# A recurrent attention and a gated feed-forward in one kernel: a new written order for all engines, with new engine choices

## The chip, the cores and the metric

The kernel runs on one core of a Trainium2 chip. Its engines work side by side, each through its own list of instructions in order: TensorE (PE in the profile; its weight loads are PEld), VectorE (DVE), ScalarE (ACT), GpSimd (POOL) and SyncE (SP), which here only issues transfers. The metric is device time in microseconds (us) of one execution, lower is better. A profile is one more execution, recorded; its span runs from the first instruction to the last.

## The reference, cut to what matters

For 4 batches, 8 heads, 768 time steps and a head size of 48, a gated linear recurrence with a complex decay, and on its output a gated feed-forward layer over 3,072 tokens of width 384:

```python
mag = np.sqrt(a_re * a_re + a_im * a_im)
scale = np.minimum(mag, 0.999) / (mag + 1e-06)
a_re_n, a_im_n = (a_re * scale, a_im * scale)
for t in range(S):
    new_re = ar * S_re - ai * S_im
    new_im = ar * S_im + ai * S_re
    kv = np.einsum('bhd,bhe->bhde', k[:, :, t], v[:, :, t])
    S_re, S_im = (new_re + kv, new_im)
    y[:, :, t] = np.einsum('bhd,bhde->bhe', q[:, :, t], S_re)
...
x = np.ascontiguousarray(attn_out.transpose(0, 2, 1, 3)).reshape(B * S, H * D)
g = x @ w_gate
gelu = 0.5 * g * (1.0 + erf(g * inv_sqrt2))
val = x @ w_val
ffn_out = gelu * val @ w_out
res_gate = 1.0 / (1.0 + np.exp(-(x @ w_res)))
return (x + res_gate * ffn_out).astype(np.float32)
```

## The kernel before, in words

**Tiling.** The recurrence is done in blocks of 128 time steps. Two such blocks (c = 0 and 1) of one batch make a group; there are 12 groups p = 0 to 11, three rounds of four batches (p % 4 is the batch, p // 4 the round). The feed-forward works on units u = 0 to 7: units 0 to 3 are the groups 0 to 3 (256 tokens each), units 4 to 7 are pairs of groups (512 tokens each).

**Steps.** All work is cut into some 1,370 named steps. A name is a kind, a group or unit, and often a block: `CP0.1.0`. Each step is one instruction, or a few of one engine, with what it reads and writes. The kinds that this document speaks of:

- Loads on SP's queue, 192 KB each (lines 525 and 889): `Lar`, `Lai` (the decay's two parts), `Lq`, `Lk`, `Lvf`.
- Gates: squares `SQI` and `SQR` (ACT or DVE), their capped sum `ADD` (DVE, 573), logarithms `LNR` and `LM`, `EXR` (ACT), the tangent of the phase `TH` (DVE, 554), `ATN` (ACT), running sums over time by matmuls `CSL` (597) and `CST` (631), exponentials `EX` and `EI`, the phase brought to one turn by `OFF` (ACT or DVE, 642), `FR` and `ABS` (DVE), then `SIN` and `COS` (ACT). All ACT functions go through one helper, line 509.
- From one round to the next: small copies through DRAM on POOL's queue (`DR` 582, `DS` 585, `DE` 605, `DI` 608, `DT` 611) and a carried phase (`CRA`, `CRB` 679, then `CDA`, `CDB` 684, accumulating transfers on POOL's queue). `MM`, `MN`, `EN` and `EB` scale the carried state (DVE, POOL or ACT).
- Products: `QE`, `KE` (696) and `QR`, `KR` (704) on DVE.
- Attention: transposes `TP` (PE) and their copies `CP` (DVE or ACT) for p below 5, above that transposing transfers `QT`, `KT` on SP's queue (709); `AT` (PE, 748), `AM` (DVE, 751), `DK` (PE, 756), `MI` and `ED` (DVE), `Y` (PE, 796 and 799), `X` (DVE or ACT). `VC` casts a value block that `Lvf` brought (520).
- Feed-forward: `XT` and `XC`, or a transposing transfer `XD` (818), bring tokens to the right layout; `GP` and `VP` (PE, 837) are the gate and value products in slices f, `GE` the GELU (ACT), `HM` their product (DVE, 848), `RP` (PE, 852) and `SG` (ACT) the output gate, `OP` (PE, 862) the output product, `OT` (DVE, 867) and `RX` (DVE or POOL, 874) the gated sum with x, `ST` the store on SP's queue (877).
- Weights on POOL's queue: `Wg0` to `Wg3`, `Wv0` to `Wv3` (909), `Wr` (912), `Wo0` to `Wo2` (915). Two tiny POOL copies, `HOLDO` and `HOLDW` (901), read a loaded `ai` tile, so POOL's list waits there for that load.

**What sets the order.** A string, `ORDER`, lists every step by hand. A loop at the end of the kernel runs through it, and each engine's list is the order of its own steps in that string. A digit behind a name's colon is the buffer that the step's tile takes. The words `log`, `trig` and `gelu` load a set of ACT's function tables. A dictionary `PARAMS['eo']` says which engine does a step that has a choice.

```python
with tc.manual_schedule():
    for nm in ORDER(st) if callable(ORDER) else ORDER.split():
        if nm in tables:
            nc.scalar.preload_act_table_set(tables[nm])
        else:
            st.run(*nm.split(":"))
```

So an instruction that waits holds all that is behind it on its engine or queue.

Of the kernel before, what the change touches and what calls it, by code (L numbers as in the profile page):

```python
# [64 lines left out]
        'CP0.0.1': 'ACT',  # L65
        'CP0.1.0': 'DVE',
# [61 lines left out]
        'MN6': 'DVE',  # L128
# [53 lines left out]
        'SQI1': 'ACT',  # L182
# [9 lines left out]
        'SQI9': 'ACT',  # L192
# [4 lines left out]
        'SQR11': 'ACT',  # L197
        'SQR2': 'DVE',
        'SQR3': 'ACT',
        'SQR4': 'ACT',  # L200
# [4 lines left out]
        'SQR9': 'ACT',  # L205
        'VC0.0': 'DVE',
        'VC0.1': 'DVE',
        'VC1.0': 'POOL',
        'VC1.1': 'DVE',
        'VC10.0': 'POOL',  # L210
        'VC10.1': 'ACT',
        'VC11.0': 'DVE',
        'VC11.1': 'POOL',
        'VC2.0': 'POOL',
# [59 lines left out]
ADD3 log LM3 Lai5.1:3 Lai4.1:4 Lk1.0:1 FR1.1 KR0.1 QE0.0 QR0.0 LNR3 TP0.0.0:20 DK0.0 EXR3 Lar2.1:0 QE0.1 CP0.0.0 SQR4
TP0.0.1:11 OFF1.0 EX1.0 MI0:0 TH3 Lai4.0 AT0.0.0:00 QR0.1 DE1:0 HOLDO CRB1 DE0:1 FR1.0 ABS1 SQI4:3 CP0.0.1 ADD4
TP0.1.1:20 AT0.0.1:11 trig SIN1:1 AM0.0.1 CP0.1.1 COS1 AM0.0.0 SQR5 DR4:0 ATN3 Lai2.0:5 Lvf0.1:1 Lar2.0 Lk1.1 Lai5.0
Lai2.1 TP0.1.0:11 Y0.0:0 X0.0 SQR2 SQI2:1 log EI1.0 ADD2 CRB0 LM2 LNR2 AT0.1.1:10 CST3.1:3 CSL3.0:200 CSL3.1:0 AM0.1.1
SQI5:0 KE1 CP0.1.0 VC0.1 AT0.1.0:01 Lq1.0:1 Lq1.1 OFF3.1 KR1 AM0.1.0 LM4 EI3.1 EI3.0 EX3.0 FR3.1 QE1 CSL2.1:111 DK0.1
# [5 lines left out]
HM0.3 VP0.1:0 Lk2.1:2 trig ATN2 Lk2.0 HM0.1 VP0.5:3 Lk3.0:3 VP0.4:0 Y1.1:3 HM0.0 ATN4 ATN5 X1.1 HM0.4 HM0.5 CST2.1:2
DK1.1 CST2.0:0 HM0.2 OFF2.1 OFF2.0 XT1.1:31 OP0.1.0:1 FR2.1 FR2.0 ABS2 KE2 SIN3:0 XC1.1 OT0.1:0 XT1.0:2 Lq2.1:2 Lq2.0
SIN2:1 OP0.0.0:0 COS2 Lq3.0:3 Lq3.1 XC1.0 KR2 COS3 GP1.5:3 GP1.0:1 GP1.2:2 OT0.0:1 QE2 Lk3.1 QR2 gelu GE1.2 GE1.5
GE1.0 Lvf2.1:1 DS4.0 CDB0 CDB1 GP1.3:0 CRB2 GP1.4:2 QE3 QR3 GE1.3 GE1.4 CSL4.0:311 TP2.0.0:10 TP2.0.1:01 Lar6.1:1
Lar6.0 Lvf2.0:0 Lar9.1:0 Lai6.0:0 CP2.0.0 CP2.0.1 log EX4.0 VP1.0:2 CST4.0:1 AT2.0.0:10 EI4.0 AT2.0.1:01 TP2.1.1:00
LM5 KE3 HM1.0 ED1 OFF4.0 CP2.1.1 CSL5.0:300 EI5.0 Lai6.1 FR4.0 AM2.0.0 EX5.0 KR3 RP1.1:2 Lai7.1:1 VC2.1:2 VC2.0 DS5.0
VP1.5:1 TP2.1.0:01 gelu SG1.1 CST5.0:3 VP1.3:2 SQR6 CP2.1.0 SQI6:2 DI4 HM1.5 AM2.0.1 CRA4 OFF5.0 FR5.0 Y2.0:4 VP1.2:1  # L290
RP1.0:3 SG1.0 Lar7.0:3 Lar7.1 AT2.1.1:10 AT2.1.0:01 CDA4 HM1.3 SQR7 GP1.1:0 VP1.1:2 CSL5.1:3 DK2.0 X2.0 ADD6 HM1.2
AM2.1.1 GE1.1 HM1.1 VP1.4:1 AM2.1.0 MI2:0 Lai8.0:5 Lai7.0 log EX5.1 LNR6 ML4 ML5 ME5 EI5.1 DR6:0 CRA5 CDA5 CST4.1:0
CSL4.1:2 SQI7:1 EX4.1 Y2.1:5 HM1.4 OFF4.1 LM6 EXR6 RX0.0 Lq4.0:0 FR4.1 RX0.1 ADD7 Lvf3.1:1 Lar9.0 TP3.0.1:10 DT4.1:0
# [677 lines left out]
```

## Time and profile before

| what | us |
|---|---|
| median of 3 runs | 273.17 |
| lowest and highest of them | 271.66, 274.95 |
| the profiled execution, its own time | 271.67 |
| span of its instructions | 269.9 |

The profile's views used here: the page's busy time per engine, with the share of the span; stage windows, which give each engine's busy time in a stretch of the span, the granted clock of TensorE and the DMA engines' share; waits, which say who waited for whom, how long in total, how often and at the longest; the chain, which goes back from the last instruction through what released each step; and groups of instructions with mean or median durations. A queue's name ends in q: SPq is SP issuing transfers.

Where steps stand in time, from the order and the timeline: unit 0's products run from 49.6 to 60.7, its `OP` from 62.8 to 68.8; unit 3's `OP` from 133.3 to 137.4; unit 7's `OP` from 257.7 to 265.6. Weights are issued at 34.7 (`Wr`) to 41.6, and from 48.3 to 57.6 (`Wo2`).

### The profile page before, as it was taken

The page shows a single profiled execution, that of the slowest core. Times are in us where ns is not written, and L with a number is a line of the kernel's source. Part 1 is how long each engine was busy: PE and PEld are TensorE (multiplying, and loading weights), DVE is VectorE, ACT ScalarE, POOL GpSimd, SP SyncE. Part 2 cuts the span into 40 slices and gives each one's busy share as a digit, 9 for nine tenths or more (in the row PEclk, how much of TensorE's full clock was granted, in tenths as well). Part 3 has the DMA queues.
Part 4 walks back from the last instruction along what each step waited for, and adds up shares of the span by engine and source line. Part 5 has one row for each costly group of instructions (what it writes and reads, how often), then busy time and mean ns, then how long its engine had stood idle before and what let it go on. Part 6 is the DMA issues. An engine that isn't in the chain of part 4 may idle for free.

```text
span 269.9 us, 5310 instructions
## 1 busy us (share of the span) xinstructions
PE 233.5 (87%) x1926; PEld 146.6 (54%) x1926; DVE 221.8 (82%) x372; ACT 213.3 (79%) x340; POOL 104.3 (39%) x149
## 2 busy tenths in 40 slices
PE   0455576997989979999997999999999999999993
PEld 0212444774757677678643466645566455654461
DVE  1736989988899999999999999988988999534633
ACT  4799999896899999999998799979969983225320
POOL 4000291632105999455487166304940611040000
PEclk9995759999999999999999999999999999999999
DMA  7999999999893799979789925992975673521002
GB/s 154 216 224 215 214 190 186 183 185 187 173 205 62 153 196 191 218 153 184 173 162 240 228 51 113 183 216 57 195 132 132 156 164 82 90 87 58 2 29 87
DMA packets 170714, 41.35 MB, mean 153 GB/s; under 512 B 162624, under 2 KB 170688, under 8 KB 170688
## 3 DMA queue, kind: packets, MB, share of 16 engines
q1 hardware_dynamic: 163200, 37.04, 67.8%
q0 software_dynamic: 7488, 3.97, 11.2%
q8 instruction: 15, 0.25, 0.4%
q14 instruction: 11, 0.09, 0.1%
HBM read 31.33 MB, written 4.76 MB: 134 GB/s over the span
## 4 chain that ended last, share of the span: by engine, by line
PE 50%; DVE 23%; ACT 10%; DMA 6%; issue 6%; SPq 4%; DVEq 0%
PE gv L837 26%; PE sums L862 7%; PE sums L852 4%; PE sums L631 4%; SPq L525 4%; DVE h L848 3%; PE at L748 3%; PE sums L597 3%; DMA ai<-in_a_im_dram 3%; ACT L938 2%; DVE atm L751 2%; ACT ai L509 2%; ACT CS L509 2%; DVE padQ L704 2%; DMA k<-in_k_dram 2%
## 5 line engine op out<-in xcount | busy, mean ns | idle before, releaser
L837 PE MATMUL gv<-xT,wv 128*128 128x256 bf16 (+1 forms) x288 | 55.1, 325 | 2.8 <-DVE h L848 2.1
L848 DVE SCALAR_TENSOR_TENSOR h<-h,gv 128x512 bf16<-128x512 bf16 x72 | 47.3, 680 | 12.3 <-PE gv L837 12.1
L509 ACT ACTIVATE h<-gv 128x512 bf16<-128x512 f32 x72 | 40.7, 599 | 20.7 <-PE gv L837 20.0
L837 PE MATMUL gv<-xT,wg 128*128 128x256 bf16 (+1 forms) x288 | 54.1, 325 | 2.1 <-DMA out_dram<-ot 0.6
L862 PE MATMUL sums<-wo,h 128*128 128x384 bf16 x288 | 49.4, 326 | 1.6 <-DMA wo<-in_moe_w_out_dram 1.6
L938 ACT ACT_TABLE_LOAD x37 | 47.5, 1283 | 1.4 <-PEq L955 0.7
L837 PEld LDWEIGHTS <-wv 128*128 128x128 bf16 x288 | 27.1, 97 | 22.4 <-issue 5.5
L837 PEld LDWEIGHTS <-wg 128*128 128x128 bf16 x288 | 27.2, 97 | 21.0 <-issue 2.8
L862 PEld LDWEIGHTS <-h 128*128 128x128 bf16 x288 | 27.6, 98 | 19.8 <-issue 2.5
L751 DVE TENSOR_TENSOR atm<-at,mask 128x512 bf16<-128x512 f32 x48 | 32.1, 680 | 0.6 <-PE at L748 0.5
L509 ACT ACTIVATE ar<-ar 128x768 f32<-128x768 f32 x31 | 25.6, 846 | 0.1
L631 PE MATMUL sums<-ai,ut 128*128 128x384 f32 x40 | 19.2, 568 | 6.1 <-ACT ai L509 5.8
L867 DVE SCALAR_TENSOR_TENSOR ot<-sg,sums 128x384 f32<-128x384 f32 x24 | 12.9, 547 | 13.7 <-PE sums L862 10.7
L520 POOL CAST v<-vf 128x384 bf16<-128x384 f32 x13 | 12.2, 942 | 21.8 <-DMA vf<-in_v_dram 21.5
L597 PE MATMUL sums<-m,ut 128*128 128x384 f32 x24 | 11.1, 546 | 10.7 <-ACT m L509 10.1
L684 POOL DMA_DIRECT2D ai<-G x16 | 14.1, 886 | 14.8 <-DVE G L679 7.7
L509 ACT ACTIVATE sg<-sums 128x384 f32<-128x384 f32 x24 | 11.6, 496 | 8.3 <-PE sums L852 7.7
L585 POOL DMA_DIRECT2D m<-d x16 | 11.8, 771 | 12.9 <-DVE M L618 7.4
L852 PE MATMUL sums<-wr,xT 128*128 128x384 bf16 x72 | 15.1, 325 | 0.4 <-DVE h L848 0.4
L611 POOL DMA_DIRECT2D m<-d x16 | 13.3, 836 | 5.3 <-DMA d<-Ei 5.3
L679 POOL TENSOR_SCALAR G<-m 32x384 f32<-32x384 f32 x8 | 11.5, 1441 | 7.8 <-issue 5.1
L509 ACT ACTIVATE m<-m 96x8 f32<-96x8 f32 (+2 forms) x29 | 13.0, 468 | 1.5 <-DVE m L573 1.3
(93 smaller groups left out, 451.7 us busy)
## 6 DMA issues: line engine op xcount, KB each, us to landing
ar<-in_a_re_dram SPq DMA_DIRECT2D x24, 192.0 KB, 3.7
ai<-in_a_im_dram SPq DMA_DIRECT2D x24, 192.0 KB, 3.8
vf<-in_v_dram SPq DMA_DIRECT2D x24, 192.0 KB, 3.7
k<-in_k_dram SPq DMA_DIRECT2D x24, 192.0 KB, 3.8
q<-in_q_dram SPq DMA_DIRECT2D x24, 192.0 KB, 3.9
out_dram<-ot SPq DMA_DIRECT2D x24, 192.0 KB, 2.4
wv<-in_moe_w_val_dram POOLq DMA_DIRECT2D x4, 288.0 KB, 11.2
wg<-in_moe_w_gate_dram POOLq DMA_DIRECT2D x4, 288.0 KB, 11.2
```

Of the source, the lines that this page charges most:

```text
L509: return nc.scalar.activation(out=out, in_=in_, func=func, **kw)
L597: st.add("CSL%d.%d" % (p, c), "PE", lambda c=c: nc.tensor.matmul(out=st["csl", (p, c)], lhsT=lmat[c], rhs=part(("m2", p), (c,)), start=Tru ...
L611: st.add("DT%d.%d" % (p, u), "POOL", lambda u=u: nc.gpsimd.dma_start(out=st["m3", p][u * D:(u + 1) * D].rearrange("p r h -> p (r h)"), in_ ...
L631: return r + [nc.tensor.matmul(out=o, lhsT=tmat[c if s == 0 else 1], rhs=part(("ai", p), (c,)), start=not both, stop=True)]
L684: st.add("CD%s%d" % (nm, p), "POOL", lambda: nc.gpsimd.dma_start(out=part(("ai", pn), (cn,))[0:1], in_=row[127:128], accum_op=OP.add), r=[ ...
L751: st.add("AM" + sfx, "DVE", lambda: nc.vector.tensor_tensor(out=st["atm", i], in0=st["at", i], in1=mask4, op=OP.mult), r=[("at", i)], w=[( ...
L837: st.add("%sP%d.%d" % (nm.upper(), u, f), "PE", lambda f=f, fs=fs, nm=nm, w=w: [nc.tensor.matmul(out=st[nm + "p", (u, f)][:, j * 256:j * 2 ...
L848: st.add("HM%d.%d" % (u, f), "DVE", lambda f=f, h2=h2: nc.vector.scalar_tensor_tensor(out=h2(), in0=h2(), scalar=0.5, in1=gv(("vp", (u, f) ...
L852: st.add("RP%d.%d" % (u, jj), "PE", lambda jj=jj: [nc.tensor.matmul(out=st["rp", (u, jj)], lhsT=st["xT", u][:, i, jj * 128:(jj + 1) * 128] ...
L862: st.add("OP%d.%d.%d" % (u, jj, hh), "PE", lambda jj=jj, fs=fs: [nc.tensor.matmul(out=st["op", (u, jj)], lhsT=st["h2", u][:, f, jj * 128:( ...
L867: st.add("OT%d.%d" % (u, jj), "DVE", lambda jj=jj: nc.vector.scalar_tensor_tensor(out=st["ot", (u, jj)], in0=st["sg", u][:, jj], scalar=1. ...
L938: nc.scalar.preload_act_table_set(tables[nm])
```

## The change

Two things in the file differ: the text of `ORDER`, and entries of `PARAMS['eo']`. No function, size, buffer count or operation is changed; the set of steps is the same.

The counts of steps per engine that differ, before and after:

| kind | before | after |
|---|---|---|
| `SQI`, `SQR` | ACT 21, DVE 5 | ACT 12, DVE 14 |
| `CP` | ACT 6, DVE 14 | ACT 8, DVE 12 |
| `OFF` | ACT 9, DVE 15 | ACT 11, DVE 13 |
| `X` | ACT 14, DVE 10 | ACT 17, DVE 7 |
| `RX` | DVE 12, POOL 12 | DVE 8, POOL 16 |
| `VC` | ACT 5, DVE 6, POOL 13 | ACT 6, DVE 7, POOL 11 |
| `EB` | ACT 5, DVE 2, POOL 1 | ACT 2, DVE 1, POOL 5 |
| `CRA`, `CRB` | DVE 8, POOL 8 | ACT 3, DVE 5, POOL 8 |
| `EN` | DVE 2, POOL 6 | DVE 3, POOL 5 |
| table sets named | 37 | 36 |

One more table load stands ahead of the first ACT instruction of the new order, which begins with a square.

The diff, cut (`...` marks what is left out):

```diff
- 'CP0.0.1': 'ACT',
- 'CP0.1.0': 'DVE',
+ 'CP0.0.1': 'DVE',
+ 'CP0.1.0': 'ACT',
...
- 'SQI3': 'ACT',
- 'SQI4': 'ACT',
- 'SQI5': 'ACT',
+ 'SQI3': 'DVE',
+ 'SQI4': 'DVE',
+ 'SQI5': 'DVE',
...
 ORDER = """
-Lar1.1:0 Lar0.1:1 log LNR0.1:0 Lar0.0 Lai0.0:0 LNR0.0 SQR0.0 SQI0.0:0 ADD0.0 Lai0.1 SQI0.1 SQR0.1 ADD0.1 EXR0.1 TH0.1
...
+Lai0.0:0 SQI0.0:0 Lar1.1:0 Lar0.0:1 log LNR0.0:0 SQR0.0 Lai0.1 Lar0.1 EXR0.0 LNR0.1 EXR0.1 SQI0.1 ADD0.0 SQR0.1
...
```

The parts of each engine's list that the prediction speaks of. POOL's queue, before:

```text
DE1 HOLDO CRB1 DE0 DR4 Wr Wv1 Wg0 Wg2 Wg3 Wg1 DS4.1 Wv3 Wv0 DR5 DE2 Wv2 VC1.0 HOLDW Wo0 Wo1 DE3 DS5.1 Wo2 DS4.0 CDB0 CDB1 VC2.1 VC2.0
```

and after:

```text
CRB0 DE0 VC0.1 DE1 HOLDW Wg2 CRB1 DR4 Wg0 Wo2 Wg1 Wg3 Wr Wv2 Wv3 HOLDO DE3 DS4.1 Wv0 Wv1 DE2 Wo0 Wo1 DR5 CDB0 DS5.0 DS4.0 DS5.1 RX0.1 CDB1 VC3.0 DI4 CRA4 CDA4 DT4.1 VC2.1
```

DVE's list up to `ADD4`, before:

```text
SQR0.0 ADD0.0 SQI0.1 SQR0.1 ADD0.1 TH0.1 TH0.0 SQR1 ADD1 OFF0.0 FR0.0 ABS0.0 TH1 VC0.0 FR0.1 ABS0.1 KE0.0 KR0.0 KE0.1 OFF1.1 VC1.1 ADD3 FR1.1 KR0.1 QE0.0 QR0.0 QE0.1 CP0.0.0 MI0 TH3 QR0.1 FR1.0 ABS1 ADD4
```

and after:

```text
SQR0.0 SQI0.1 ADD0.0 SQR0.1 ADD0.1 TH0.0 TH0.1 SQI1 SQR1 ADD1 OFF0.0 SQI3 FR0.0 OFF0.1 FR0.1 ABS0.1 TH1 KE0.0 SQR2 ABS0.0 KE0.1 KR0.1 SQR3 KR0.0 ADD3 ADD2 QE0.1 QR0.1 SQR4 QE0.0 QR0.0 FR1.1 FR1.0 TH3 CP0.0.0 CP0.0.1 ABS1 SQI4 ADD4
```

SP's queue, the loads 20 to 50, before:

```text
Lar3.0 Lq0.0 Lar4.0 Lai5.1 Lai4.1 Lk1.0 Lar2.1 Lai4.0 Lai2.0 Lvf0.1 Lar2.0 Lk1.1 Lai5.0 Lai2.1 Lq1.0 Lq1.1 Lvf1.0 Lk2.1 Lk2.0 Lk3.0 Lq2.1 Lq2.0 Lq3.0 Lq3.1 Lk3.1 Lvf2.1 Lar6.1 Lar6.0 Lvf2.0 Lar9.1 Lai6.0
```

and after:

```text
Lai2.1 Lai2.0 Lar4.1 Lq1.0 Lq0.0 Lai4.1 Lar4.0 Lar5.0 Lk1.0 Lai5.0 Lai4.0 Lai5.1 Lk1.1 Lar5.1 Lq1.1 Lar7.0 Lvf1.0 Lvf1.1 Lk2.1 Lk2.0 Lvf2.0 Lq2.0 Lq2.1 Lq3.0 Lq3.1 Lk3.0 Lvf2.1 Lk3.1 Lar7.1 Lvf3.0 Lai7.1
```

Further on, SP's list before has `Lvf3.0 Lai9.1 ST0.0 Lq4.1 Lai8.1`; after, `Lk6.0 Lk4.1 ST0.1 Lvf3.1 Lk5.0`, with `ST0.0` behind group 5's first `XD`. PE's list has the same matmuls in another order; in both, `OP0.1` and `OP0.0` stand ahead of all of unit 1's products, and they read all three `Wo`.

More of the change, by code (lines that the diff above doesn't have):

```diff
@@ L127 @@
         'MN5': 'POOL',
-        'MN6': 'DVE',
+        'MN6': 'POOL',
         'MN7': 'POOL',
@@ L181 @@
         'SQI0.1': 'DVE',
-        'SQI1': 'ACT',
+        'SQI1': 'DVE',
         'SQI10': 'ACT',
@@ L191 @@
         'SQI8': 'ACT',
-        'SQI9': 'ACT',
+        'SQI9': 'DVE',
         'SQR0.0': 'DVE',
@@ L196 @@
         'SQR10': 'ACT',
[L197 removed]
+        'SQR11': 'DVE',
         'SQR2': 'DVE',
[L199 to L200 removed]
+        'SQR3': 'DVE',
+        'SQR4': 'DVE',
         'SQR5': 'ACT',
@@ L204 @@
         'SQR8': 'ACT',
[L205 to L208, printed above, removed]
+        'SQR9': 'DVE',
+        'VC0.0': 'ACT',
+        'VC0.1': 'POOL',
+        'VC1.0': 'DVE',
         'VC1.1': 'DVE',
[L210 to L214, printed above, removed]
+        'VC10.0': 'ACT',
+        'VC10.1': 'DVE',
+        'VC11.0': 'ACT',
+        'VC11.1': 'DVE',
+        'VC2.0': 'DVE',
         'VC2.1': 'POOL',
@@ L274 @@
[L274 to L278, printed above, removed]
@@ L284 @@
[L284 to L288, printed above, removed]
@@ L289 @@
[L289 to L293, printed above, removed]
@@ new lines @@
+FR0.1 ABS0.1 TH1 Lar3.0:2 Lk0.1 trig ATN1 Lvf0.1:1 Lar2.1:3 Lar2.0 Lar3.1 KE0.0 COS0.1:0 SIN0.0 SIN0.1 SQR2 ABS0.0
+CST1.0:0 CSL1.0:111 COS0.0 KE0.1 KR0.1 SQR3 KR0.0 ADD3 Lai2.1:3 Lai2.0 SQI2:3 ADD2 QE0.1 Lar4.1:1 Lq1.0:1 Lq0.0
+Lai4.1:4 CST1.1:2 CSL1.1:3 QR0.1 Lar4.0 SQR4 log EI1.0 LM3 QE0.0 Lar5.0:0 EX1.0 CRB0 DE0:0 QR0.0 TP0.0.0:10 EX1.1
+OFF1.0 OFF1.1 FR1.1 LNR3 EXR3 VC0.0:0 EI1.1 LM2 FR1.0 TH3 VC0.1 DE1:1 TP0.0.1:21 Lk1.0:1 Lai5.0:5 Lai4.0 CP0.0.0
+CP0.0.1 ABS1 CSL2.1:300 Lai5.1 HOLDW Lk1.1 AT0.0.1:00 DK0.0 AT0.0.0:11 TP0.1.1:01 SQI4:0 ADD4 Lar5.1 Lq1.1 AM0.0.1
@@ new lines @@
+CDB0 KR2 CRB2 ED1 GP1.4:3 Lq2.0:2 Lq2.1 QE2 OT0.0:1 Lq3.0:3 Lq3.1 Lk3.0:3 GE1.4 GP1.3:2 QR2 GE1.3 QE3 RP1.0:1 VP1.0:0
+SG1.0 DS5.0:1 DS4.0 DS5.1 CSL4.0:300 TP2.0.0:20 log EI4.0 ML5 LM5 QR3 EX4.0 HM1.0 CP2.0.0 Lvf2.1:0 TP2.0.1:11 CP2.0.1
+CSL4.1:0 Lk3.1 Lar7.1 KE3 KR3 CST4.0:2 DK2.0 EI4.1 EX4.1 AT2.0.1:00 CSL5.0:311 VP1.5:1 OFF4.0 EX5.0 EI5.0 SQR7 FR4.0
+Lvf3.0:1 RX0.0 HM1.5 AT2.0.0:11 TP2.1.1:01 Lai7.1:0 Lar6.1:0 Lar6.0 Lai6.1:2 Lai6.0 CP2.1.1 RX0.1 AM2.0.1 VP1.1:3
+AM2.0.0 CDB1 CST5.0:2 OFF5.0 TP2.1.0:10 Y2.0:4 SQR6 SQI6:2 ML4 Lq8.1:0 X2.0 CP2.1.0 VC3.0:3 DI4 CRA4 CDA4 DT4.1:0 ME4
@@ new lines @@
+HM1.1 FR5.0 MI2:0 ADD6 CSL5.1:0 VP1.2:3 VP1.4:2 AT2.1.0:00 AT2.1.1:11 AM2.1.0 AM2.1.1 Lvf4.0:1 Lai7.0 EX5.1 EI5.1
+SQI7:3 Lk4.0:0 Lar8.0:3 LNR6 VC2.1 DK2.1 VP1.3:1 XT2.0:00 Y2.1:5 XC2.0 HM1.3 HM1.4 CST4.1:0 EXR6 HM1.2 TP3.0.1:10
+RP1.1:2 TH6 ADD7 CRA5 DE4:4 X2.1 CP3.0.1 DT4.0 DR6:0 CDA5 OP1.0.0:3 gelu SG1.1 OFF4.1 FR4.1 AT3.0.1:00 TP3.0.0:21
+AM3.0.1 ED2 CP3.0.0 DI5 TP3.1.1:10 log ME5 ABS4 LM6 CST5.1:0 OT1.0:2 CP3.1.1 LNR7 Lar8.1 XT2.1:2 AT3.0.0:11 XC2.1
+AM3.0.0 OFF5.1 FR5.1 Lar9.1:1 Lk6.0:1 OP1.1.0:1 Lk4.1 ST0.1 DK3.0 GP2.3:3 Y3.0:6 EXR7 TP3.1.0:21 Lvf3.1:0 GP2.5:0
```

277 lines of the change are left out of this document (139 added, 138 removed).

## Prediction

> **What bounds the kernel now.** I read the page's busy totals first, then the stage windows, the waits, and the chain of waits. The page:
>
> ```profile
> PE 233.5 (87%) x1926; PEld 146.6 (54%) x1926; DVE 221.8 (82%) x372; ACT 213.3 (79%) x340; POOL 104.3 (39%) x149
> ```
>
> Three engines lie within 21 us of each other, so the average names no bound. By stage (columns: window, its length, then busy us of PE, PEld, DVE, ACT, POOL, TensorE's clock, DMA share, GB/s):
>
> ```profile
> 0.00:20.00 20.00, 6.74 (x10) 2.59 (x10) 8.53 (x21) 14.59 (x23) 4.00 (x15) 0.99 1.01 198
> 20.00:40.00 20.00, 12.21 (x71) 8.01 (x72) 16.50 (x29) 19.25 (x27) 7.84 (x11) 0.59 1.12 206
> 40.00:60.00 20.00, 16.83 (x180) 12.61 (x180) 18.98 (x31) 18.67 (x32) 8.23 (x14) 1.00 1.27 185
> 60.00:80.00 20.00, 17.73 (x158) 12.51 (x156) 17.62 (x27) 16.36 (x26) 3.83 (x6) 1.00 1.04 188
> 80.00:100.00 20.00, 18.35 (x209) 14.17 (x209) 19.90 (x36) 19.84 (x31) 15.39 (x20) 1.00 0.79 132
> 100.00:120.00 20.00, 19.33 (x204) 14.76 (x200) 19.87 (x33) 19.92 (x33) 13.18 (x19) 1.00 0.97 194
> ...
> 220.00:240.00 20.00, 20.00 (x192) 12.11 (x190) 13.31 (x23) 6.93 (x13) 2.95 (x5) 1.00 0.51 101
> ```
>
> The reader should see three regimes. Until 80 us PE waits (26.5 us idle) while the DMA engines are full. From 80 to 120, ACT and DVE are full and PE nearly. At the end PE alone is full. PE's work is the same in both kernels, so the end moves only by what PE's idle time loses.
>
> Inside the first regime, first two of the waits (who waited for what: us in total, times, longest), then three pieces of the chain (start, length, what):
>
> ```profile
> POOL v L520 <- DMA vf<-in_v_dram: 21.5, 5, 9.4
> ...
> PE sums L862 <- DMA wo<-in_moe_w_out_dram: 1.6, 1, 1.6
> ```
>
> ```profile
> 61.34 4.03 SPq L525
> ...
> 66.39 0.63 SPq L525
> ...
> 68.32 3.26 DMA ai<-in_a_im_dram
> ```
>
> An SP load issues every 0.6 to 1.2 us, but 4 to 5 us apart from 40.7 to 65.5. The packet records say why: from 36.3 to 64.9 us the weights' queue and the loads' queue move one packet each in turn, some 200 per us per queue, against 1,150 per us for loads alone. A load (1,024 packets of 192 bytes) then takes 5 us. The last weight (Wo2) lands at 65.8, and PE stands 1.62 us for it inside OP0.
>
> **The weights.** Before, DR4 waits for ADD4 (ends 33.93); eight weights follow at 34.72, four more from 48.3 to 56.9; the queue has no gap. In the new order one (Wg2) stands ahead of DR4; seven follow DR4, two DE3, two DE2. So 384 of the 4,992 weight packets go early, and the two DS5 copies no longer stand among the weights. If ADD4 ends when it did, 4,900 packets (weights and small copies) instead of 5,470 at 192 per us take 25.5 instead of 28.5 us: last landing 62.7 instead of 65.8.
>
> Does ADD4 end when it did? I added row durations along each queue. Ahead of ADD4 DVE has 4.7 us more medians (SQI1, SQI3, SQR2 to SQR4, ADD2, QE0.0 and others stand earlier or come from ACT). Before, DVE idles 14.6 us ahead of it, so there is room. SQR4 now waits for Lar4.0, SP's 26th load; the 26th was issued at 22.4 and loads land in 3.7, so SQR4 ends at 27.1. Behind it stand QE0.0 .74, QR0.0 .56, FR1.1 and FR1.0 .5 each, TH3 .95, two CP of .65, ABS1 .5, SQI4 and ADD4 .95 each: 34.0. Bounds: 33.9 (no delay) and 39.5 (none of the idle time used); I take 34.0, for each wait in that list has its source earlier.
>
> Start: ACT now squares first, and its log table load (rows: 1,283 ns), hidden before behind the first load's landing (ACT idle 2.67 us), stands after SQI0.0, from 4.7 to 6.0. It is covered: LM0.1 waits for ADD0.1 either way (9.4 before, 9.2 now). Cost 0; 1.3 without that cover.
>
> PE then: OP0.1 starts at 62.7, both OP0 take 3.9, then seven groups of .65, one of .49 and CSL4.0 .7: TP2.0.0 at 72.3, with 38.1 us of PE work ahead of it (row sums, overlap of neighbours left out). Before: 72.7, with 36.3. Lead: 0.4 + 1.8 = **2.2 us** (0 if ADD4 is at its late end, 4 if the weights are hidden whole).
>
> **Engine choices.** Counts from the two lists, by row means. ACT loses 5 SQI and 4 SQR (9 x .835), 3 EB (1.5) and one table set (1.28; the extra load at the start is idle time), and gains 2 CP (2.0), 2 OFF (1.2), 3 X (1.4), 1 VC (.5) and 3 CR: -3.7 net. CR has no ACT row; bounds .36 (DVE's CR) and .52 (ACT's 96x384 cast); I take .5, as it is ACT's. DVE gains 9 squares (.95 each) and loses 2 CP, 2 OFF, 4 RX, 3 X, 3 CR and some steps under .55: +1.5. POOL gains 4 RX (.97 each), 4 EB (.5) and loses 2 VC (.94) and small steps: +3.6. The squares move mostly before 45 us, where DVE has idle time. Between OP0.0 and OP3.0 (66.7 to 135.3, 68.6 us), the row sums of all that must precede a step, by data or by queue, grow by 63.9 for ACT instead of 64.7, and for DVE by about 63.2 instead of 64.3: **-0.8** (bounds 0 and -1.5).
>
> **SP's queue.** Before, ST0.0 stands ahead of Lq4.1 and waits for RX0.0:
>
> ```profile
> SPq L877 <- DVE ot L874: 37.4, 6, 17.3
> ```
>
> SP issues nothing from 80.6 to 88.3, and Lq4.1's landing is on the chain. Now ST0.0 stands behind unit 4's transposes, and ST0.1, in front, waits for POOL's RX0.1, which comes when OT0.1 (65.2) and three DS copies are through, by 69. PE idles 1.65 us from 80 to 100; I take half, **-0.8** (0 to -1.65). Some five loads get through beside the weights in either order; now Lq2, Lq3 and Lk3 are behind them and land by 68, at .9 each once the weights are done. Their readers QE3 and KE3 come at 70 and 73: 0. Without that margin, each late us is a us of DVE.
>
> **POOL's queue.** VC2.1 moves behind CRA4 (1.2), CDA4 (.8) and DT4.1 (.8), and PE's DK2.1, with VP1.3, Y2.1 and CST4.1 behind it, waits for VC2.1. FR4.0 at 75.5 gives VC2.1's end at 78.8; PE comes there at 81. Cover 2 us; DT4.1's wait for a landing can be 2.9 (longest of its line). DVE and POOL also collide:
>
> ```profile
> L520 DVE CAST Gb<-G x2: 349/1288/2226, 144.0 to 218.8; 96x384 bf16<-96x384 f32 x2
> ```
>
> The same cast takes 349 ns, and 2,226 at 143.96, beside POOL's VC7.0 and RX3.1. Two-input DVE rows hardly stretch: TH 970 on the mean, 947 median. So I give **+0.5** for both (0 to 2.4: 0.9 late for VC2.1, 1.5 for collisions). The Trainium skill ("SBUF — State Buffer", section "SBUF: two separate sides") says that the shared port pair is an exclusive lock for a whole instruction, also between a two-input DVE operation and a GpSimd one that reads SBUF. By that rule alone the added 3.6 us of POOL work could stop DVE for their whole length, and the sum below would be -0.2 instead of -3.3; the cast row agrees, the two-input rows do not.
>
> **Sum.** -2.2 - 0.8 - 0.8 + 0.5 = -3.3. The profiled execution took 271.67 (span 269.9 and 1.8 around it), so 268.4. The median of the three runs shown, 273.17, is 1.0055 of it: **269.9**. From 190 us on PE has 73.4 us of work and took 75; nothing is changed there.
>
> **Rivals.**
>
> *The lead is given back.* For: in 80 to 140 ACT, DVE and PE are all at 97% or more, DVE gets 1.5 us more, and VC2.1's place is tight. Against: ACT has less, PE's work there shrinks by what was done earlier. Price: -2.2 + 1.5 (all of DVE's) + 0.9 (VC2.1) - 0.8 = -0.6, so 271.1, or 272.6 by the median's scale.
>
> *Collisions at full length.* Every added us of POOL's elementwise work stops DVE, as in the cast row. Price: -3.3 - 0.5 + 3.6 = -0.2: 271.5, or 273.0. For: one row of six times its length. Against: the means of the HM and AM rows, 680 ns, are their medians. These two end within 1%. The lock of the Trainium skill's page "SBUF — State Buffer", above, would make this case the likeliest; the rows leave it the least.
>
> *Slower: ADD4 comes late.* DR4 holds seven weights behind a DVE that now has 4.7 us (with full-length squares 5.1) more to do. If the early waits leave it none of its 14.6 us, ADD4 ends at 39.5 and the last weight lands at 68.2; OP0, which is in front of all of unit 1 on PE, starts 5.4 later than before, less the 1.6 it stood: +3.8. With -0.8 from ACT: 274.7, or 276.2. It decides from ADD4 at about 38 us. For: the queues are in order, and Lar4.0 stands four places later in SP's. Against: the walk above.
>
> That the change does nothing is out: every engine's list differs.
>
> **Chances.** Forecast 0.53, given back 0.19, collisions 0.06, slower 0.22. About 1% is what a measurement here can tell from no change, 270.4 to 275.9. Of the forecast's own range (266 to 271.5) 0.07 lies above 270.4; of the slower case 0.02 lies under 275.9. Faster 0.46, same 0.34, slower 0.20. The range: at the low end all terms at their far ends (-4 -1.5 -1.65 = -7.2, so 264.5, or 266 scaled) and a little under, as PE's 26.5 idle us leave room: 264.5; at the high end the slower case: 277.
>
> **What would show it.** Right: a profile with ADD4's DVE instruction near 34, Wg2's issue before 28, the PE wait for wo ending at 63 or earlier, no hold of SP near 80 to 88, PE idle until 80 us near 23. Wrong: the first seven weights issued after 38; a PE wait for v or padK near 80; DVE casts of over 1 us; SP loads of 5 us whose readers wait; idle PE after 140, where I expect none new.

## The result, and the profile after

| | us | runs |
|---|---|---|
| before, median (lowest to highest) | 273.30 (271.66 to 274.95) | 20 |
| after, median (lowest to highest) | 275.19 (272.82 to 277.31) | 20 |
| after, the profiled execution (span) | 275.17 (273.4) | 1 |

After to before the ratio is 1.0066, 95% interval 1.0041 to 1.0091: 1.8 us slower, less than 1% but clear of the noise. I had forecast 269.9; the time lies inside my range of 264.5 to 277, on the other side of no change. Before's profiled execution, 271.67, was one of its fastest, after's an average one, so the spans differ by 3.5 us and the medians by 1.8.

The page after:

```profile
PE 235.8 (86%) x1913; PEld 147.5 (54%) x1926; DVE 229.3 (84%) x368; ACT 210.9 (77%) x339; POOL 108.7 (40%) x154
```

ACT lost 2.4 us (forecast 3.7), POOL gained 4.4 (3.6). DVE gained 7.5 where I had counted 1.5: its rows became longer. The stage windows after, and one of before that the prediction does not show:

```profile
20.00:40.00 20.00, 13.22 (x77) 8.74 (x78) 18.31 (x28) 18.92 (x29) 7.77 (x11) 0.79 1.04 189
40.00:60.00 20.00, 16.40 (x159) 11.38 (x157) 16.11 (x26) 17.29 (x28) 7.53 (x12) 0.95 1.27 188
60.00:80.00 20.00, 17.88 (x159) 13.27 (x160) 17.49 (x27) 18.05 (x28) 6.73 (x8) 1.00 1.03 181
...
140.00:160.00 20.00, 16.75 (x105) 8.57 (x109) 19.53 (x25) 15.27 (x28) 8.14 (x13) 1.00 1.01 190
```

```profile
140.00:160.00 20.00, 17.58 (x130) 9.41 (x130) 19.34 (x27) 16.38 (x32) 9.37 (x14) 1.00 0.90 192
```

From 40 to 60 PE, DVE and ACT all do less than before (16.8, 19.0 and 18.7 there): something none of them makes is late. From 140 to 160 DVE is full and PE has lost another 0.8 us against before. The chain says what was late first (start, length, what):

```profile
38.22 10.29 DMA wg<-in_moe_w_gate_dram
...
48.80 11.90 DMA wv<-in_moe_w_val_dram
...
60.74 0.84 PE gv L838 x6
```

and the waits between 55 and 70 us agree:

```profile
PEld L838 <- DMA wv<-in_moe_w_val_dram: 1.7, 1, 1.7
DVE h L849 <- PE gv L838: 1.7, 1, 1.7
PE gv L838 <- DMA wv<-in_moe_w_val_dram: 1.5, 1, 1.5
```

The wait for `wo` that the prediction started from is gone. PE stands for `wv` instead: `VP0.2` starts at 60.7 when Wv1 lands, against 51.9 before. `OP0.1` then starts at 65.8, not 62.7. The last weight, Wo1, was late as well (the issues of the three `Wo`, and their time to landing):

```profile
L916 POOL DMA_DIRECT2D wo<-in_moe_w_out_dram x3: 742/778/814, 37.4 to 54.8; - x3
...
DMA to landing us min/median/max: 9.0/10.6/11.3
```

Issued at 54.8, it lands at 66.1. `OP0.1` came to Wo1's slices at 66.4, so in this execution the value weights and the last landing were nearly level.

The second place is at 150 us; waits between 144 and 156, then the rows of the two lines that meet at 142, with the same K line before in between (counts; shortest, median and longest in ns; first and last start):

```profile
ACT sg L510 <- PE sums L853: 3.6, 1, 3.6
PEld L853 <- issue: 2.7, 1, 2.7
PE sums L853 <- DVE h L849: 2.4, 1, 2.4
```

```profile
L705 DVE TENSOR_TENSOR padK<-CS,kE x2: 958/1924/2889, 142.0 to 149.0; 128x1536 bf16<-128x1536 bf16 x2
L705 DVE TENSOR_TENSOR padQ<-CS,qE x2: 957/1212/1466, 146.4 to 152.7; 128x1536 bf16<-128x1536 bf16 x2
```

```profile
L704 DVE TENSOR_TENSOR padK<-CS,kE x2: 948/953/958, 143.1 to 149.5; 128x1536 bf16<-128x1536 bf16 x2
```

```profile
L875 POOL TENSOR_TENSOR ot<-ot,x x2: 917/922/927, 142.2 to 143.0; 128x384 f32<-128x384 f32 x2
```

`KR6` takes 2.89 us instead of 0.96 while POOL runs RX3.1 and RX3.0; `HM4.10`, behind it on DVE, comes late, and PE's `RP4.1`, which takes the buffer that `HM4.10` reads, stands 2.44 us for it until 152.3.

To see where the end was lost I read off when PE had done a given sum of its own work (row medians of before, along each kernel's own PE list). The last three columns are runs told below:

| PE's work done, us | before | after | RX3 on DVE | Wo2 last | best version |
|---|---|---|---|---|---|
| 29 (in unit 0's `OP`) | 64.1 | 66.3 | 65.3 | 61.8 | 61.9 |
| 32 (unit 0's `OP` done) | 68.4 | 69.5 | 68.4 | 65.3 | 66.2 |
| 45 | 82.8 | 84.0 | 82.9 | 79.9 | 80.1 |
| 85 | 125.6 | 127.1 | 126.0 | 123.1 | 123.2 |
| 109 | 152.6 | 155.3 | 151.8 | 152.0 | 149.0 |
| 117 | 160.6 | 164.0 | 161.5 | 160.0 | 157.8 |
| 221 (unit 7's last `OP`) | 263.3 | 266.7 | 265.3 | 263.1 | 260.9 |

The first row lies ahead of the 1.6 us for which PE stands for Wo2 in the kernel before (64.2 to 65.8), so its 2.2 us are too much. When unit 0 is done, after is 1.1 us behind; it loses 0.4 from there to 85 and 1.9 from 85 to 117. Behind that, nothing.

### The profile page after: what moved, and what is told of

The parts are those of the page before. It is cut to its first block, busy times and chain, and to the rows that moved or that the text cites. A ratio compares the mean times of both kernels' runs of the same rounds, so it can differ in the third digit from the quotient of the medians.

```text
span 273.4 us, 5296 instructions
## 1 busy us (share of the span) xinstructions
PE 235.8 (86%) x1913; PEld 147.5 (54%) x1926; DVE 229.3 (84%) x368; ACT 210.9 (77%) x339; POOL 108.7 (40%) x154
## 4 chain that ended last, share of the span: by engine, by line
PE 44%; DMA 18%; DVE 11%; ACT 11%; issue 6%; SPq 6%; POOL 2%; DVEq 0%; ACTq 0%; POOLq 0%
PE gv L838 19%; PE sums L863 13%; SPq L526 5%; DMA wv<-in_moe_w_val_dram 4%; DMA wg<-in_moe_w_gate_dram 4%; DMA ar<-in_a_re_dram 3%; PE sums L853 3%; ACT L939 2%; DMA ai<-in_a_im_dram 2%; PE sums L632 2%; PE sums L598 2%; ACT m L510 2%; PE at L749 2%; ACT ar L510 2%; ACT CS L510 1%
## 5 line engine op out<-in xcount | busy, mean ns | idle before, releaser
L838 PE MATMUL gv<-xT,wv 128*128 128x256 bf16 (+1 forms) x281 | 54.3, 324 | 2.4 <-DMA wv<-in_moe_w_val_dram 1.9
L838 PE MATMUL gv<-xT,wg 128*128 128x256 bf16 (+1 forms) x282 | 52.1, 324 | 2.4 <-DMA xT<-x 0.8
L510 ACT ACTIVATE h<-gv 128x512 bf16<-128x512 f32 x72 | 40.0, 601 | 13.9 <-PE gv L838 13.2
L838 PEld LDWEIGHTS <-wg 128*128 128x128 bf16 x288 | 27.5, 98 | 20.8 <-issue 1.9
L875 POOL TENSOR_TENSOR ot<-ot,x 128x384 f32<-128x384 f32 x16 | 18.4, 1151 | 47.8 <-DVE ot L868 47.7
L510 ACT ACTIVATE ar<-ar 128x768 f32<-128x768 f32 x27 | 22.6, 849 | 0.1
L685 POOL DMA_DIRECT2D ai<-G x16 | 13.3, 830 | 22.5 <-ACT ai L510 16.3
L598 PE MATMUL sums<-m,lt 128*128 128x384 f32 x24 | 12.4, 603 | 9.1 <-ACT m L510 9.1
L680 POOL TENSOR_SCALAR G<-m 32x384 f32<-32x384 f32 x8 | 10.8, 1355 | 22.4 <-DVE m L646 13.8
L632 PE MATMUL sums<-ai,ut 128*128 128x384 f32 x40 | 18.5, 547 | 0.6 <-DVE m L646 0.5
L705 DVE TENSOR_TENSOR padK<-CS,kE 128x1536 bf16<-128x1536 bf16 (+1 forms) x13 | 14.6, 1122 | 0.5
```

What stands on the lines that cost most here:

```text
L510: return nc.scalar.activation(out=out, in_=in_, func=func, **kw)
L598: st.add("CSL%d.%d" % (p, c), "PE", lambda c=c: nc.tensor.matmul(out=st["csl", (p, c)], lhsT=lmat[c], rhs=part(("m2", p), (c,)), start=Tru ...
L632: return r + [nc.tensor.matmul(out=o, lhsT=tmat[c if s == 0 else 1], rhs=part(("ai", p), (c,)), start=not both, stop=True)]
L705: return nc.vector.tensor_tensor(out=pad, in0=st["CS", p][:, cs[0] * H:(cs[-1] + 1) * H], in1=sb, op=OP.mult)
L838: st.add("%sP%d.%d" % (nm.upper(), u, f), "PE", lambda f=f, fs=fs, nm=nm, w=w: [nc.tensor.matmul(out=st[nm + "p", (u, f)][:, j * 256:j * 2 ...
L875: st.add("RX%d.%d" % (u, jj), rese, lambda jj=jj, pc=(p, c), eng=eng: eng.tensor_tensor(out=st["ot", (u, jj)], in0=st["ot", (u, jj)], in1= ...
```

## The experiments

Ratios are to the kernel before, run beside each on the same chip. Ten were made from the changed kernel (1.0066), three from the kernel before.

### Wo2 last (e1)

```diff
-FR3.0 ABS3 Wg0 Wo2 Wg1 Wg3 ...
+FR3.0 ABS3 Wg0 Wg1 Wg3 ...
-... VP0.4:2 Wo1 Y1.1:3 ...
+... VP0.4:2 Wo1 Wo2 Y1.1:3 ...
```

> The changed kernel with one weight moved: Wo2 goes from the third place behind DR4 to the last place of the weights, so that Wv0 and Wv1 come one place (384 packets of 768 bytes) earlier. Theory V (the value weights are late): in the changed kernel VP0.2 stands until 60.7 us for Wv1 and OP0.1 starts at 65.8 although all of Wo has landed by then. At some 200 packets per us Wv1 lands 1.9 us earlier, VP0.2 starts near 58.8 and OP0.0 ends near 67.6 instead of 69.5; if two thirds of that lasts to the end, the time is about 1.3 us lower than the changed kernel's 275.2, so 273.9. Rival L (only the last landing counts): the last weight lands as before, near 64, and OP0.1, which needs all twelve, ends no earlier; no change, 275.2. Rival E (the engines' backlog holds unit 0): VP0.2 starts earlier and OP0.0 does not; no change.

Measured: 271.18, ratio 0.9931 (0.9910 to 0.9953). One transfer moved takes the changed kernel from slower than before to faster, by 1.35% of the time. Waits between 55 and 70, and two windows:

```profile
PE sums L863 <- DMA wo<-in_moe_w_out_dram: 0.4, 1, 0.4
```

```profile
40.00:60.00 20.00, 17.54 (x189) 13.56 (x188) 17.93 (x30) 19.36 (x29) 6.04 (x9) 0.96 1.27 185
60.00:80.00 20.00, 18.29 (x162) 13.09 (x161) 18.27 (x29) 18.39 (x31) 8.97 (x11) 1.00 1.07 196
```

The wait for `wv` is gone, a short one for `wo` is back, and the three engines do more again from 40 to 60. Wv1 lands at 54.8 (60.7 after; 58.5 in the run with RX3 on DVE, whose order is the same up to there), `OP0.0` ends at 65.3 (69.5; 68.4). Theory V holds, and the gain is more than my 1.3, which counted Wo2 as 384 packets; it has 512. Up to 2 us of the 4.2 between the two profiles came from the start of the weights (34.6 here, 36.7 after), which differs between executions of the same order. Rival L is settled by two later profiles that differ in Wo2's place alone, both with RX3 on DVE (e3 and e5 below): the last weight lands at 63.7 in one and 63.9 in the other, but unit 0 is done at 68.4 with Wo2 third and at 66.3 with Wo2 last, and the ratios are 0.9999 and 0.9943.

### Six weights ahead of DR4 (e2)

```diff
-... EXR2 DR4:0 TP1.0.0:31 ...
+... EXR2 Wg0 Wg1 Wg3 Wr Wv2 Wv3 DR4:0 TP1.0.0:31 ...
```

> The changed kernel with Wg0, Wg1, Wg3, Wr, Wv2 and Wv3 moved ahead of DR4, so that they no longer wait for ADD4 (which ends at 35.7 us). They are issued from about 31.5 us. Theory H (the wait for ADD4 is what makes the weights late): the weights start some 5 to 7 us earlier and Wv1 lands near 55; OP0.0 ends 2 to 3.5 us earlier and the time is 273.0 (1.5 to 3 lower than 275.2). Rival S (the wait shields the loads): beside the weights a load takes 5 us instead of 1; five or six loads land later by up to 7 us each, units 0 and 1 get their inputs late, and what VP0.2 gains is lost ahead of it: 275 to 277.

Measured: 278.05, ratio 1.0191 (1.0154 to 1.0228). Rival S. The chain and a wait:

```profile
34.43 15.37 DMA vf<-in_v_dram
```

```profile
PE sums L632 <- ACT xT L520: 6.1, 1, 6.1
```

A load of v is 15.4 us on the chain, stuck beside the weights; DVE does nothing from 38 to 42, and PE stands 6.1. So the wait for ADD4, which I had priced as a risk, shields the loads.

### RX3.0 and RX3.1 on DVE (e3)

```diff
-        'RX3.0': 'POOL',
-        'RX3.1': 'POOL',
+        'RX3.0': 'DVE',
+        'RX3.1': 'DVE',
```

> The changed kernel with RX3.0 and RX3.1 on DVE instead of POOL. In the changed kernel the DVE row KR6 takes 2.89 us instead of 0.96 while POOL runs RX3.1, RX3.0 and CDB4, and QE6 and QR6 take 1.47 each beside POOL's EB6, DS8.1 and EN7. Theory C (the bf16 two-input DVE rows stand while POOL reads or writes the on-chip memory): KR6 is back near 1.0, DVE does 1.1 to 1.4 us of RX more and 1.9 less in KR6; PE's idle 2.44 us at 152.3 falls to about 1.5, and the time is lower by 0.5 to 1, 274.4. If POOL's rows then move forward and meet other DVE rows, the gain is smaller. Rival B (KR6 is long for another reason, and DVE's own sum is what counts): DVE has 1.1 to 1.4 us more, KR6 stays long, and the time goes up by about 1 us, 276.2.

Measured: 272.88, ratio 0.9999 (0.9968 to 1.0031), 1.8 us under the changed kernel. Groups of instructions between 132 and 160 us (busy, mean ns of one, idle before):

```profile
L752 DVE TENSOR_TENSOR atm<-at,mask 128x512 bf16<-128x512 f32 x6 | 3.8, 680 | 0.0
L705 DVE TENSOR_TENSOR padQ<-CS,qE 128x1536 bf16<-128x1536 bf16 x2 | 2.4, 1212 | 0.1
...
L705 DVE TENSOR_TENSOR padK<-CS,kE 128x1536 bf16<-128x1536 bf16 x2 | 2.1, 1026 | 0.2
```

padK's mean falls from 1924 to 1026; padQ, which stands beside POOL's `EB6` and `EN7`, is as it was. Theory C, and twice what I expected.

### Wg2 behind DR4 (e4)

```diff
-... AM0.0.0 Wg2 CRB1 ...
+... AM0.0.0 CRB1 ...
-... EXR2 DR4:0 TP1.0.0:31 ...
+... EXR2 DR4:0 Wg2 TP1.0.0:31 ...
```

> The changed kernel with Wg2 moved from ahead of CRB1 to just behind DR4, where the others stand. Theory S2 (the early weight slows the loads that ADD4 waits for: between 30 and 33 us only 1,644 load packets move instead of some 3,200, and Lk1.1 takes 2.8 us): Lai4's load lands up to 1.4 us earlier, SQI4 no longer waits 0.5, ADD4 ends 0.5 to 1 earlier; but Wv1 stands 384 packets further back, +1.9, so VP0.2 starts 1 to 1.4 later: time 275.2 to 276.2. Rival G (the early weight is a plain gain): ADD4 as it was, VP0.2 1.9 later, time 276.5.

Measured: 273.48, ratio 1.0015 (0.9989 to 1.0041): not slower, as both theories had it, but 1.4 us faster than the changed kernel, with intervals that just touch. The packet records show what makes up for the later place: the loads, no longer slowed at 30 to 33, get so far ahead that their queue is all but empty from 39 to 47 (SP waits for a v buffer), and there the weights move 240 to 268 packets per us instead of 200. Wv1 lands at 58.0, though it stands one weight further back (60.7 after; 58.5 in both e3 and e8, which have Wg2 early). Where the 1.4 us come from is not shown: unit 0 is done at 68.1, between e3's 68.4 and e8's 67.6. The early weight, which I had counted as a gain, is none.

### The parts that I had priced: SP's hold, squares, late RX

Before, with one store moved twice:

```diff
-... Lvf3.0:0 Lai9.1:2 ST0.0 Lq4.1 ...
+... Lvf3.0:0 Lai9.1:2 Lq4.1 ...
+... Lk7.0:2 ST0.1 ST0.0 Lq8.1:3 ...     (first run)
+... QE4 Lai9.0 ST0.0 Y3.0:6 ...         (second run)
```

> The kernel before with one store moved: ST0.0 goes from ahead of Lq4.1 to behind ST0.1, so that SP no longer stands 7.8 us (80.6 to 88.3) for RX0.0 with eleven loads behind it. The prediction's step: the load Lq4.1 and those behind it come up to 8 us earlier, PE loses up to 1.65 us less between 80 and 100, I took 0.8: 272.1 against 272.9. Rival (covered): the readers of these loads (KE4, QE4, QR4) stand behind DVE's own full list at 80 to 120 and would run no earlier; 272.9, within 0.3.

Measured: 279.31, ratio 1.0223 (1.0192 to 1.0255). Loads came 6.5 to 7.9 us earlier, and every DVE row up to 96 us kept exactly its distance (0.5) to before. Then:

```profile
DVE ot L867 <- DMA out_dram<-ot: 3.6, 1, 3.6
```

`OT1.1` takes the buffer that `ST0.0` empties, so the later store held DVE. That spoils the run as a test of the end, so the store was put where it goes out on time:

> The kernel before, with ST0.0 behind Lai9.0 instead of ahead of Lq4.1: the seven loads from Lq4.1 to Lai9.0 come 7 to 8 us earlier, while the store itself goes out when it did (88 us), so that OT1.1, which takes the store's buffer, is not held as it was (3.6 us) with the store behind ST0.1. The prediction's step: 0.8 lower, 272.2. Rival (covered: with the store behind ST0.1 the same loads came as early, and every DVE row up to 95 us kept its distance): 273.0, within 0.3; and if the loads behind Lai9.0 come earlier as well, not before Lvf4.0's own wait (93.0 us).

Measured: 274.02, ratio 1.0032 (1.0006 to 1.0058). No gain: the loads came 5.4 to 6.9 us earlier, the DVE rows up to 97 us again kept their distance (0.5), so the hold of 7.8 us was covered.

The changed kernel with nine squares back on ACT (`'SQI1': 'ACT'` and so on):

> The changed kernel with the nine squares that went to DVE (SQI1, 3, 4, 5, 9, SQR3, 4, 9, 11) back on ACT, their places in the order kept. DVE loses 8.6 us of work, ACT gains 7.5, six of the nine before 45 us. The prediction's step (they cost DVE nothing there, and ACT is worth 0.8 between units 0 and 3): the front is later, as ACT has 18.9 of 20 us in 20 to 40, by 1 to 3 us, and the middle by up to 2: 276.5 to 279. Rival D (DVE's list is what makes ADD4 and the weights late): ADD4 ends near 33, the weights start 1 to 2 us earlier, 273.5 to 275.

Measured: 277.04 (three runs), ratio 1.0136 (1.0114 to 1.0158), 1.9 us over the changed kernel. The squares are better on DVE, as the prediction had it.

The changed kernel with the ten RX of units 4 to 7 back:

> The changed kernel with the ten RX steps of units 4 to 7 that the change moved between DVE and POOL back where they were (seven on DVE, three on POOL). The rows KR9 and KE11, stretched by 0.55 and 0.68 beside RX4.0 and RX5.1, are then short. Theory F (from 165 us on PE has no gap, so nothing that DVE and POOL do there moves the end): 275.2, within 0.4; only the last rows (RX7.1, RX6) could move the tail, by 0.3. Rival (collisions count there too): 274.0; or DVE's 3 to 4 us more cost in the tail: 276.

Measured: 275.41, ratio 1.0087 (1.0057 to 1.0118), no difference to the changed kernel, in whose profile PE has no gap of over 0.25 us from 165 us on. In this run's profile it has two, 0.66 and 1.12.

### Both repairs, and three ways to keep RX3 off KR6

Wo2 last and RX3 on DVE (e5):

> The changed kernel with both repairs: Wo2 last among the weights, and RX3.0 and RX3.1 on DVE. Alone they brought 271.2 and 272.9 us against about 275.2. With Wo2 last alone PE still stands 2.57 us at 147.5, behind a KR6 of 2.88 us. Theory C (POOL's two RX rows stretch the DVE row beside them): KR6 near 1.1, PE's stand near 0.9, time 269.0 to 270.0, below both kernels. Rival B (the two repairs overlap: with unit 0 earlier, DVE's sum sets the middle and RX on DVE costs 1.1 to 1.4): 271 to 272.

Measured: 271.68, ratio 0.9943 (0.9915 to 0.9970): no better than Wo2 last alone. `KR6` is 0.96, but `QR6` now takes 2.03 and the two RX take 0.9 us of a DVE that has no gap from 144 to 160. So RX3 stayed on POOL, behind EB7 (e9):

```diff
-... DS8.0:0 RX3.1 RX3.0 CDB4 ...
+... DS8.0:0 CDB4 ...
-... EB7:0 CDA8 ...
+... EB7:0 RX3.1 RX3.0 CDA8 ...
```

> Wo2 last among the weights, and RX3.1 and RX3.0 stay on POOL but stand behind EB7 (POOL idle from 147.8 to 158.2 in the changed kernel) instead of beside KR6. DVE gets no RX (in the run with both repairs it had 1.1 to 1.4 us more and nothing was won). Theory C2 (the collision costs, and the RX on DVE cost as much again): KR6 near 1.0, QE6 and QR6 still stretched by POOL's EB6 and EN7, which come forward by 1.9 us; PE's stand at 147.5 (2.57 with Wo2 last alone) falls to about 1; 269.7 to 270.5 against 271.2 to 271.7. Rival D (DVE's own list sets 140 to 158, with or without the collision): 271 to 271.7, no better than Wo2 last alone.

Measured: 271.77, ratio 0.9947 (0.9922 to 0.9972). PE's stand near 147 fell from 2.57 to 0.68, but a new one of 0.99 came at 156. Another row had walked into the RX, DVE's `CRA8` (timeline: start, us, engine, line):

```profile
153.76 1.56 DVE L680 TENSOR_SCALAR G<-m 32x384 f32<-32x384 f32 x1
```

The same with Wg2 behind DR4 (e10):

> The same, and Wg2 behind DR4. With Wg2 behind DR4 alone the time was 273.5 (1.4 to 1.7 under the changed kernel): between 39 and 48 us the loads' queue was empty, and the weights moved 240 to 268 packets per us instead of 200, so that Wv1 landed no later (57.5 against 58.6 in a run of the same front). Theory Q (the early weight only changes places with loads): the last weight lands near 63, OP0.1 stands for it by 0.5 to 1, time as without this move, within 0.5. Rival P (the loads that get ahead of the weights are worth something further on): 0.7 to 1.4 lower, 269.

Measured: 270.44, ratio 0.9919 (0.9892 to 0.9947), not told apart from 0.9947. Last, the RX behind CDA8, which needs `CRA8` (e12):

> As the last version (Wo2 last, Wg2 behind DR4, RX3.1 and RX3.0 on POOL behind EB7), but with the two RX behind CDA8 too. In the last version they met DVE's CRA8, which took 1.55 us instead of 0.50, and PE stood 0.98 us at 155.3. CDA8 needs CRA8, so now they cannot meet it: the DVE rows beside them are AM6, HM4 and OFF9. Theory T (only some DVE rows are stretched beside RX: the bf16 products KE, KR, QE, QR, the bf16 casts and CRA; HM, AM, OFF are not): CRA8 0.50, PE's stand at 155 gone, 0.5 to 1 lower: 269.5 to 270. Rival U (any DVE row is stretched): AM6 or HM4 take 1.2 us or more, no gain, 270.4.

Measured: 270.05, ratio 0.9897 (0.9872 to 0.9921). This is 1% under the kernel before and beats both kernels. Its timeline while POOL runs three RX from 154.0 to 157.0:

```profile
152.86 0.36 DVE L680 TENSOR_SCALAR G<-m 32x384 f32<-32x384 f32 x1
153.25 0.69 DVE L849 SCALAR_TENSOR_TENSOR h<-h,gv 128x512 bf16<-128x512 bf16 x1
153.85 1.28 DVE L752 TENSOR_TENSOR atm<-at,mask 128x512 bf16<-128x512 f32 x2
155.05 0.68 DVE L849 SCALAR_TENSOR_TENSOR h<-h,gv 128x512 bf16<-128x512 bf16 x1
155.65 0.55 DVE L643 TENSOR_SCALAR m<-sums 128x384 f32<-128x384 f32 x1
```

Theory T: `CRA8` is 0.36 again and no DVE row beside the RX is long. These rows (HM, AM, OFF) take an operand from a matmul's result; `KR`, `QR`, `QE` and `CRA`, which are stretched, do not. The step from 0.9919 to 0.9897 is within the intervals; that the stand at 155 is gone, the profile shows.

### A value weight late in the kernel before (b3)

```diff
-... DE2:2 Wv2 GP0.5:2 ...
+... DE2:2 GP0.5:2 ...
-... Wo0 Wo1 DE3:3
+... Wo0 Wo1 Wv2 DE3:3
```

> The kernel before, with Wv2 moved two places back among the weights, behind Wo0 and Wo1; Wo2 stays last, so the last landing stays at 65.4. By the landings of the profile before, Wv2 then lands at 60.5 instead of 56.4. Theory V (a value weight's place sets unit 0): VP0.3, which started at 57.5, stands until 60.6; OP0.1 starts at 65.8 and no longer stands 1.6 us for Wo2; OP0.0 ends 1.5 later, time 1 to 1.5 higher, 274.2 to 274.7. Rival L (only the last landing counts): 273.2.

Measured: 279.33, ratio 1.0226 (1.0199 to 1.0253). The last weight lands at 66.0 (65.4 before), and `OP0.0` ends 6.7 us later. Theory V, outside the new order too. My size was too small, for two reasons. Two places back is 63.0 by the landings in the profile before (a `Wo` is 384 KB, the others 288), not 60.5. And PE, having stood 5.6 us, came back at a lower clock (columns as above):

```profile
58.00:62.00 4.00, 0.01 (x1) 0.00 (x0) 0.52 (x1) 3.38 (x4) 1.99 (x4) 1.00 1.27 185
62.00:66.00 4.00, 2.41 (x12) 1.74 (x13) 0.69 (x1) 0.00 (x0) 0.63 (x1) 0.59 1.26 194
```

The work from `VP0.3` to `Y1.1`, 2.9 us before, took 4.9.

## Why the prediction was wrong, point by point

**The weights (forecast -2.2): the step that failed.** "OP0.1 starts at 62.7" was read off the last landing alone. The order *among* the weights changed as well: Wo2, which unit 0 needs last, went from the last place to the third, and Wv0 and Wv1, which `VP0` needs first, went behind it. I listed that order and did not walk its landings against the matmuls that wait for each. The nine weights from Wg0 to Wv1 are 3,584 packets; in after's profile the first moves at 38.8 and the last at 58.7, Wv1's landing is signalled at 60.7, and from `VP0.2` to `OP0.1` PE has 5 us of work: 65.8. The other inputs of the walk held in part. ADD4 was put at 34.0; in the seven profiles whose order is the same up to there it ends at 33.7 to 35.7 (after's is the latest). The last landing was put at 62.7; it is 62.9 to 63.9 in e1, e5 and e9, where Wo2 is last, but 63.7, 64.5 and 66.1 in e3, e8 and after. `TP2.0.0` was put at 72.3: 71.6 to 72.3 with Wo2 last (e1, e5, e9), 74.2 to 75.9 without (e8, e3, after). Unit 0 is done at 65.3 to 66.3 in the five profiles with Wo2 last, where the forecast comes to 66.6, and at 69.5, 68.4 and 67.6 in after, e3 and e8 (before: 68.4, with the same PE work ahead of it). With Wo2 last, unit 0 ends 2.4 us behind the last landing in all five; in after, e3 and e8 it ends 1.0, 2.3 and 0.7 later than that, and this is the value weights' part. The rest is the last landing's own: in after, at 66.1, it alone would have undone the lead. At this mark the term is +1.1, 0 and -0.8, some +0.1 where -1.8 was forecast: about 2 us of the miss.

**Wg2 ahead of DR4.** Issued at 27.5, as forecast, but counted as packets saved. With it behind DR4, Wv1 landed no later (e4).

**Start (0).** Right: `LM0.1` starts at 9.3 after and 9.4 before.

**Engine choices (-0.8): no gain shows.** From unit 0's end to 85 us of PE's work, before takes 57.2 us; after and its two relatives of the same order (e3, e8) take 57.6, 57.6 and 58.1. The gain forecast for SP's queue falls into the same stretch, so there 1.6 were to be won, and some 0.5 were lost. The squares by themselves are worth 1.9 (e7); which of the other choices took that back, no run shows.

**SP's queue (-0.8): wrong.** The hold is covered (b_st0_later, b2): the loads' readers stand behind DVE's own list. It is 0.8 of the miss, inside the stretch just named. `ST0.0` also had a second reader of its place, the buffer for `OT1.1`, which I did not name.

**POOL's queue (+0.5): the mechanism right, the size wrong.** VC2.1 ended at 85.4 instead of 78.8 and cost nothing, since PE came there at 86.5. The collisions cost more. Summed over all DVE rows more than 0.1 us above the median of their kind in the two profiles together, the excess is 9.4 us after and 4.0 before; most of it lies elsewhere, but 3.0 of it is between 140 and 148 (before: 1.4), and taking RX3 away gave 1.8. I had weighed the row that was six times its length against HM, AM and TH, which "hardly stretch"; HM and AM are no witnesses, as the last version shows, and the mean of TH was none either: in the profile before, one of its eleven rows ran beside a POOL row, and that one took 1.20 instead of 0.95. In 14 profiles together (all runs but e7), 34 of the 40 TH rows beside a POOL row are longer, up to 1.87 us, and none of 163 HM and 173 AM rows is. The Trainium skill ("SBUF — State Buffer", section "SBUF: two separate sides") says that two-input operations lock when both inputs are in SBUF, and that a perf-mode operation locks too. The prediction had left the place of the inputs out. The traces agree with the skill for the rows that were stretched, `KR6` by 1.9 us, and for HM and AM, which were not; in which mode `CRA8` runs, no run shows. Applied to the rows it speaks of, the rule would have told which DVE steps to look at beside each RX.

**No idle PE after 140: wrong**, 2.44 us at 152.3.

**Rivals.** "Slower: ADD4 comes late" came nearest in time (276.2), but its mechanism happened only in part: ADD4 was 1.7 us late and the last landing 3.4, yet ADD4 stayed below the 38 us from which it was to decide. So its time came near by luck. "Collisions at full length" was part of what happened; I gave it 0.06. "The lead is given back" can be seen in the version with Wo2 last: by the table it is 3.1 us ahead when unit 0 is done, 2.5 at 85 and 0.6 at 109, behind the long `KR6`; the best version is still 2.8 ahead at 117. (From 80 to 140 before, PE was at 96%, not at 97% or more.) Together: -3.3 + 2.0 + 2.1 (engine choices and SP's queue) + 1.3 (collisions 1.8 instead of 0.5) = +2.1; measured +1.8. Each term differs by 1 us or more between profiles, and the profile before, against which they are read, was 1.6 us under its median, so a sum this close is no proof of its parts.

What stays open: why the run-to-run spread of the start (ADD4 within 2 us for one order) is as wide as it is; why after's weights took 29.4 us from Wg0's issue to the last landing, against 28.1 to 28.6 in e1, e3, e5, e8 and e9; and how much of the collision's 1.8 us is left once Wo2 is last, since there each cure but the last moved the collision to another row.

## What to carry to other kernels

When a queue of transfers is reordered, walk every transfer's landing against the first instruction that needs it; the last landing is only one of the ends. When two kernels are compared by the work done, read behind a stand that one of them is known to have, not ahead of it. A wait that holds a bulk queue back can be what keeps the small transfers fast, so price what it protects before counting it as a cost. Before giving elementwise work to POOL, look at which DVE rows stand beside it at that place: some kinds can be held for POOL's whole instruction, others were never held, and a cure that only shifts the overlap has to be read off the next profile.

## What the runs showed of the hardware that was not expected

- Two queues with packets of 768 and 192 bytes share by packets, not by bytes: about 200 per us each, so a 192 KB load takes 5 us beside the weights, and six weights issued earlier (from 30.2 us in e2, 36.7 in after) cost 3.4 us. The Trainium skill ("DMA: Bandwidth & Descriptors", section "Queues, rings and completion order") says that each DMA engine takes turns between queues packet by packet; the records agree. Alone, the weights moved 240 to 268 packets per us, only a quarter more.
- One DVE row can be held by several POOL instructions in a row: `KR6` 2.89 us for 0.96, beside two RX of 0.92 each; `CRA8` 1.56 for 0.36. Which one is held goes mostly by which began first: all 34 long TH rows of 14 profiles began behind the POOL row, while 18 KE rows that began ahead of an RX kept 0.9 to 1.0 us, and the RX beside them took 1.1 to 1.6 instead of 0.92. `KR6` is an exception: its record begins 0.16 us ahead of RX3.1.
- Behind a stand of 5.6 us PE's granted clock was 0.59 (b3, 62 to 66). Stands of 1.5 and 2.4 us (after, until 60.7 and 152.3) left it at 1.00 in the windows that hold them; one of 2.6 (e1, until 147.5) lies in a window with 0.91 (140 to 160).
